# A fixed TensorE order for an attention stage, with its value products one step later

## Chip, cores, metric

One core of a Trainium2 chip runs the whole program. The metric is the device time of one execution in microseconds (us). Below, PE is TensorE, DVE VectorE, ACT ScalarE, POOL GpSimd, and SP the engine that issues the DMAs.

## What is computed

Attention with a causal window of 128 over 4 batches, 8 heads, 576 positions of width 64; then a mixture of 8 experts whose gate is normalised over rows and columns eight times; then a two-layer network with a leaky rectifier. Cut to the stage that the change touches:

```python
scores = q @ k.T / 8 + bias          # per batch and head; bias = -slope[h] * distance
scores = where(0 <= distance < 128, scores, -1e9)
attn = exp(scores - max) ; attn = attn / (attn.sum(-1) + 1e-9)
x = (attn @ v) laid out as (2304, 512)
P = softmax-like gate of x @ w_gate  # 2304 x 8
out = sum over e of P[:, e] * (relu(x @ w1[e]) @ w2[e])
```

## The kernel before

The 2304 tokens are 18 tiles of 128. Attention takes 36 **steps**: tile i, heads 0 to 3 (`quad` 0), then heads 4 to 7 (`quad` 1). Steps are numbered s = 0 to 35, so tile i has steps 2i and 2i+1. A step has four pieces of TensorE work, named here by a letter; all of it is fp32, and the profile shows each fp32 product as two instructions where it uses half of the array.

- **S**, `scores` (L238): four products of 64 rows, eight instructions. Heads of odd and even number lie in the upper and the lower 64 partitions, so that two products that follow each other use different halves of the array's rows. DVE then adds the bias and finds the minimum (L243), ACT does the exponential (L247).
- **T**, `probs_T` (L273): eight transposes of 128 by 128 into two PSUM tiles `pt`; ACT copies each to SBUF as `pb` (L275).
- **V**, `values` (L288): eight products with `v`, sixteen instructions, whose outputs alternate between the lower and the upper 64 partitions. After `quad` 1, DVE multiplies the tile's sums by the inverses and writes `acc[i]` (L296).
- **R**, the second half of `inverses` (L260), once per tile: the inverse row sums are spread over partitions by sixteen instructions, and ACT copies them to `rb` (L263).

In program order a step s issues S of step s+1, then some jobs of a list `fill`, then T of step s (and R at `quad` 1), more of `fill`, and V of step s. `PAIRS` groups the tiles: pairs 0, 1 and 2 are tiles 0 to 3, 4 to 7 and 8 to 11. When a pair's four tiles are done, its `acc` tiles are added and split into two fp16 parts (`XP[p]`, by ACT at L427 and POOL at L428 and L474), and `fill` gets its fourteen products with the first weights (`a_steps`, L702, six instructions each), its gate products (`logits`, L327) and, for pairs 0 and 1, its fourteen products with the second weights (`b_steps`, L819). The same list holds, in steps 0 to 7, the preparation of the first chunk of both weights, W[0][0] and W[1][0]: the largest magnitude (`largest`, four ACT squares each, L550), a scale factor for it (`scale_jobs`: small DVE operations and two small PE products that share one PSUM bank with the other factors), the scaling on ACT (L553), and seven fp16 splits with four sums between them (`whole`: ACT L427, POOL L428 and L577). The k-th product of `a_steps` needs split k of W[0][0], and from the third product on also the sums and the last split of `XP[p]`.

The order on every engine is made by the framework at build time: it takes instructions by program order as their inputs come ready in its own timing of the kernel, and each engine then runs its list in order. So the TensorE order of before is not the program's: pieces are broken up and mixed. An explicit edge without a semaphore (`add_manual_dep` with `NoSync`) forces one instruction behind another in that list.

After step 35 come the inputs of pairs 3 and 4, the gate, and for the remaining 1700 us the products of all chunks.

Of the kernel before, what the change touches and what calls it, by code (L numbers as in the profile page):

```python
# [13 lines left out]
AF = mybir.ActivationFunctionType  # L14
ALU = mybir.AluOpType
# [11 lines left out]
FIRST = (0, 1, 3)  # L27
# [4 lines left out]
def attn_moe_kernel(  # L32
# [81 lines left out]
    pools = {}  # L114

    anchors = {}

    def anchor():
        ins = nc.cur_bb.bb.instructions[-1]
# [93 lines left out]
    def load_v(i):  # L213
        v_t = ap3.tile([P, DM], F32, tag="v", name="v_t")
        nc.sync.dma_start(v_t, v[i * P:(i + 1) * P, :])
        st[i]["v"] = v_t
# [6 lines left out]
    def scores(i, quad):  # L223
        c = st[i]
        kb, qs = c["kb"], c["qs"]
        W = P * len(kb)
        c0 = 2 * P - W
        mn = ap2.tile([P, 4], F32, tag="mn", name="mn")
        if quad == 0:
            c["sm"] = ap2.tile([P, H], F32, tag="sm", name="sm")  # L230
        sm = c["sm"]
        s = [ps_s.tile([P, 2, 2 * P], F32, tag="s", name="s") for _ in range(2)]
        e = [ap1.tile([P, 2, 2 * P], F32, tag="e", bufs=5, name="e") for _ in range(2)]
        c[quad] = dict(e=e)
        for n in range(2):
            for r in range(2):
                h = 4 * quad + 2 * n + r
                nc.tensor.matmul(s[r][:, n, 0:W], qs[64 * r:64 * r + 64, h // 2, :],  # L238
                                 c["k"][64 * r:64 * r + 64, h // 2, 0:W], start=True, stop=True)
        for n in range(2):  # L240
            for r in range(2):
                h = 4 * quad + 2 * n + r
                nc.vector.tensor_tensor_reduce(  # L243
                    out=e[r][:, n, 0:W], in0=s[r][:, n, 0:W], in1=c["bias"][:, c0:], scale=2.0 ** (-8.0 * (h + 1) / H),
                    scalar=float(2**41), op0=ALU.add, op1=ALU.min, accum_out=mn[:, 2 * n + r:2 * n + r + 1],
                )
                nc.scalar.activation(  # L247
                    out=e[r][:, n, 0:W], in_=e[r][:, n, 0:W], func=AF.Exp, bias=mn[:, 2 * n + r:2 * n + r + 1],
                    scale=-1.0, accum_out=sm[:, h:h + 1],
                )  # L250

    def inverses(i):

        c = st[i]
        sm = c["sm"]
        nc.scalar.activation(out=sm, in_=sm, func=AF.Copy, bias=EPS)
        nc.vector.reciprocal(out=sm, in_=sm)
        rt = ps_t.tile([P, NP, P], F32, tag="pt", name="rt")
        for h in range(H):
            nc.tensor.matmul(rt[64 * (h % 2):64 * (h % 2) + 64, h // 2, :], sm[:, h:h + 1].to_broadcast([P, D]), ident,  # L260
                             start=True, stop=True)
        rb = c["rb"] = ap1.tile([P, NP, P], F32, tag="rb", name="rb")
        nc.scalar.activation(out=rb, in_=rt, func=AF.Copy)  # L263

    def probs_T(i, quad):
        c = st[i][quad]
        nb = len(st[i]["kb"])
        c["pb"] = []
        for r in range(2):
            pt = ps_t.tile([P, 2, 2, P], F32, tag="pt", name="pt")  # L270
            for n in range(2):
                for b in range(nb):
                    nc.tensor.transpose(pt[:, n, b, :], c["e"][r][:, n, b * P:(b + 1) * P], ident)  # L273
            pb = ap3.tile([P, 2, 2, P], F32, tag="pb", name="pb")
            nc.scalar.activation(out=pb[:, :, 0:nb, :], in_=pt[:, :, 0:nb, :], func=AF.Copy)  # L275
            c["pb"].append(pb)

    def values(i, quad):
        kb = st[i]["kb"]
        if quad == 0:  # L280
            st[i]["o"] = ps_o.tile([P, NP, P], F32, tag="o", name="o")
        o = st[i]["o"]
        pb = st[i][quad]["pb"]
        for n in range(2):
            for b, j in enumerate(kb):
                for r in range(2):
                    h = 4 * quad + 2 * n + r
                    nc.tensor.matmul(  # L288
                        o[64 * r:64 * r + 64, h // 2, :],
                        st[j]["v"][:, h * D:(h + 1) * D],  # L290
                        pb[r][:, n, b, :],
                        start=(b == 0), stop=(b == len(kb) - 1),
                    )
        if quad == 1:
            p = max(p for p, (t0, n) in enumerate(PAIRS) if t0 <= i)
            nc.vector.scalar_tensor_tensor(out=accT[i], in0=o, scalar=xin[p].sr[:, 0:1], in1=st[i]["rb"],  # L296
                                           op0=ALU.mult, op1=ALU.mult)
# [18 lines left out]
    def logits(p):  # L316

        t0, n = PAIRS[p]
        lp = ps_a.tile([P, 2, n, 2 * E], F32, tag="s1", name="lp")

        first = [(0, wgs, 0), (1, wgs, 2)]
        second = [(0, wgs, 0), (2, wgs, 2), (5, wgn, 0)]
        for s, terms in enumerate((first, second)):
            for k in range(n):
                todo = [(o, w, k0, i) for o, w, k0 in terms for i in range(4)]
                for m, (o, w, k0, i) in enumerate(todo):
                    nc.tensor.matmul(lp[:, s, k, :], XP[p][:, o, i // 2, i % 2, k * P:(k + 1) * P], w[:, k0 + i // 2, :],  # L327
                                     start=(m == 0), stop=(m == len(todo) - 1))
        back = small.tile([P, 1], F32, tag="lb", bufs=1, name="lb")
        nc.scalar.activation(out=back, in_=xin[p].sr[:, 1:2], func=AF.Copy, scale=srg[:, 1:2])  # L330
        to = Pm[:, t0:t0 + 2 * n, :].rearrange("p (s k) e -> p s k e", s=2)
        nc.scalar.activation(out=to, in_=lp[:, :, :, 0:E], func=AF.Copy, scale=back)
        nc.vector.scalar_tensor_tensor(out=to, in0=lp[:, :, :, E:2 * E], scalar=back, in1=to, op0=ALU.mult, op1=ALU.add)
# [105 lines left out]
    class Inputs:  # L439
# [18 lines left out]
        def largest(self, k):  # L458
            nc.vector.tensor_reduce(out=self.mx[:, k:k + 1], in_=acc[self.t0 + k], axis=AX.X, op=ALU.max,
                                    apply_absolute_value=True)  # L460
# [75 lines left out]
    class Weights:  # L536
# [9 lines left out]
            nc.sync.dma_start(self.raw, chunks[self.ci][self.which].rearrange("(k p) f -> p k f", p=P))  # L546

        def largest(self, k):
            junk = stg.tile([P, FC], BF16, tag="junk", bufs=1, name="junk")
            nc.scalar.activation(out=junk, in_=self.raw[:, k], func=AF.Square, accum_out=self.mx[:, k:k + 1])  # L550

# [1 line left out]
            nc.scalar.activation(out=self.raw[:, k], in_=self.raw[:, k], func=AF.Copy, scale=self.sr[:, 0:1])  # L553

        def scale(self):
            jobs = [lambda k=k: self.largest(k) for k in range(KT)] + scale_jobs(self.mx, KT, self.sr, squares=True)
            jobs += [lambda k=k: self.scaled(k) for k in range(KT)]
            if self.which == 1:
                jobs.append(self.back)
            return jobs  # L560
# [106 lines left out]
    def a_steps(ci, p):  # L667
# [6 lines left out]
        def step(g, j, d):  # L674
# [22 lines left out]
            for f in range(nf):  # L697
                ft = g * nf + f
                i = 0
                for kk in range(2):  # L700
                    for wp, xp in ((0, 0), (0, 1), (1, 0)):
                        nc.tensor.matmul(d[b][:, f, :], t[:, wp, kk, ft * P:(ft + 1) * P], XP[p][:, o, kk, xp, :],  # L702
                                         start=(i == 0 and f == 0 and j in FIRST), stop=(i == 5), skip_group_check=True)
                        i += 1
            ps = d[b].rearrange("p f t -> p (f t)")

# [91 lines left out]
    def b_steps(ci, p):  # L798
# [5 lines left out]
        def step(tt, j, d):  # L804
# [11 lines left out]
            for ft in range(2):  # L816
                h, f = Ht[ci, p, ft]
                for hp, wp in ((0, 0), (0, 1), (1, 0)):
                    nc.tensor.matmul(ps, h[:, o, hp, f, tt * P:(tt + 1) * P], w[:, wp, ft, :],  # L819
                                     start=(i == 0 and j in FIRST), stop=(i == 5), skip_group_check=True)  # L820
                    i += 1
            t, half = ((ta, 0), (ta, 0), (ta, 1), (tb, 1), (tb, 1), (ta, 1), (tb, 0))[j]
            dst = acc[t][:, half * HF:(half + 1) * HF]
# [64 lines left out]
    def filling(left):  # L888
        for f in [fill.pop(0) for _ in range(min(-(-len(fill) // max(left, 1)), len(fill)))]:
            if f is not None:  # L890
                f()
            tick()

    for s, (i, quad) in enumerate(steps):
# [11 lines left out]
        if s + 1 < len(steps):  # L906
            if quad == 1 and i + 2 < NTILE:
                load_qk(i + 2)
            if quad == 0 and 2 <= i + 1 < NTILE:
                load_v(i + 1)  # L910
            scores(*steps[s + 1])
        if quad == 0 and i + 5 < NTILE:
            largest_v(i + 5)
        for p, (t0, n) in enumerate(PAIRS):
# [2 lines left out]
        filling(left)  # L917
        if scales:
            scales.pop(0)()
        probs_T(i, quad)  # L920
        if quad == 1:
            inverses(i)
        filling(left - 1)
        if scales:
            scales.pop(0)()
        values(i, quad)
    assert not fill
    for _ in range(8):
        tick()
    actx.close()  # L930
# [150 lines left out]
```

## Time and profile before

| | |
|---|---|
| three runs | 1959.19, 1960.06, 1962.14 us; median 1960.06 |
| the profiled execution | 1959.59 us; its span 1957.8 us |
| PE busy over the span | 1890.2 us (97%), 17725 instructions |
| DVE, ACT, POOL busy | 1320.9 (67%), 1366.5 (70%), 1327.3 us (68%) |
| mean granted TensorE clock | 0.995 |

A busy PE is not a PE at its peak: two products in different halves of the array can run side by side, and the busy time does not tell whether they do. Times inside the kernel count from the span's start.

### The profile page before, as it was taken

The numbers are of one execution on the slowest core, as the hardware profiler recorded it, in microseconds if no ns is written. First come the engines' busy times: TensorE is split into PE (matmuls) and PEld (weight loads), VectorE is DVE, ScalarE is ACT, GpSimd is POOL, SyncE is SP. The second block draws the span as 40 slices with busy tenths as digits, with TensorE's granted clock in tenths as the row PEclk, the third lists the DMA queues.
The fourth block names the chain that finished last, engine by engine and source line by source line (L and its number), as shares of the span: only waits on it lengthen the run. The fifth ranks groups of instructions, "written<-read, shape, count | busy, mean of one in ns | idle before, by whom it ended". The sixth has DMA issues, their size and how long they took to land.

```text
span 1957.8 us, 45103 instructions
## 1 busy us (share of the span) xinstructions
PE 1890.2 (97%) x17725; PEld 1626.5 (83%) x17725; DVE 1320.9 (67%) x3604; ACT 1366.5 (70%) x3123; POOL 1327.3 (68%) x1142
## 2 busy tenths in 40 slices
PE   8999988999999999999999999999999998999998
PEld 6777667888898888889888888889889877889897
DVE  6444466676776767677676767666666777677876
ACT  7977666776767666676767676676666778776764
POOL 3843275868787786878677686775767686666743
PEclk9999999999999999999999999999999999999999
DMA  8432001120211211120111112101000000001001
GB/s 269 125 87 71 12 12 55 39 62 32 82 47 47 66 39 55 39 82 28 66 65 40 55 39 66 44 2 45 23 23 23 23 23 23 24 22 44 2 28 71
DMA packets 57861, 97.80 MB, mean 50 GB/s; under 512 B 3632, under 2 KB 22064, under 8 KB 57648
## 3 DMA queue, kind: packets, MB, share of 16 engines
q1 hardware_dynamic: 57648, 94.92, 14.9%
q8 instruction: 138, 2.26, 0.5%
q14 instruction: 75, 0.61, 0.1%
HBM read 81.81 MB, written 13.11 MB: 48 GB/s over the span
## 4 chain that ended last, share of the span: by engine, by line
PE 78%; ACT 7%; DVE 5%; DMA 5%; POOL 3%; issue 2%; POOLq 0%; SPq 0%; ACTq 0%; DVEq 0%
PE t L819 35%; PE s L702 21%; PE sq L702 15%; DMA raw<-in_moe_w_dram 3%; PE s L238 2%; PE o L288 2%; PE pt L273 1%; ACT junk L550 1%; POOL h L775 1%; DVE s L731 1%; PE rt L260 1%; ACT raw L553 1%; ACT w L427 1%; ACT e L247 1%; ACT xp L427 1%
## 5 line engine op out<-in xcount | busy, mean ns | idle before, releaser
L819 PE MATMUL t<-w,h 128*128 128x256 f16 x7560 | 985.1, 273 | 22.9 <-ACT part L829 10.3
L702 PEld LDWEIGHTS <-w 128*128 128x128 f16 x8400 | 759.1, 98 | 120.3 <-issue 35.0
L819 PEld LDWEIGHTS <-h 128*128 128x128 f16 x7560 | 730.2, 98 | 125.6 <-issue 33.9
L702 PE MATMUL s<-xp,w 128*128 128x256 f16 (+1 forms) x4908 | 620.3, 263 | 20.3 <-ACT q L726 10.4
L832 DVE SCALAR_TENSOR_TENSOR acc<-t,pu,acc 128x256 f32<-128x256 f32 x864 | 407.9, 479 | 220.3 <-PE t L819 173.3
L775 POOL TENSOR_TENSOR h<-s,h 128x1024 f16<-128x1024 f32 x180 | 388.2, 2157 | 136.8 <-ACT h L772 95.7
L702 PE MATMUL sq<-xp,w 128*128 128x256 f16 (+1 forms) x3492 | 447.5, 262 | 6.2 <-ACT q L714 4.5
L830 POOL TENSOR_TENSOR acc<-acc,part 128x256 f32<-128x256 f32 x324 | 235.6, 729 | 292.9 <-ACT part L829 260.6
L428 POOL TENSOR_TENSOR w<-raw,w 128x512 f16<-128x512 f32 x240 | 277.7, 1168 | 42.3 <-ACT w L427 41.9
L731 DVE SCALAR_TENSOR_TENSOR h<-sq,h 128x512 f16<-128x512 f32 (+1 forms) x348 | 190.6, 552 | 82.4 <-ACT h L756 47.6
L829 ACT ACTIVATE part<-t,pu 128x256 f32<-128x256 f32 x324 | 152.5, 471 | 109.0 <-PE t L819 100.1
L772 ACT ACTIVATE h<-s 128x1024 f16<-128x1024 f32 x180 | 189.6, 1053 | 42.2 <-DVE s L731 41.3
L718 DVE SCALAR_TENSOR_TENSOR sq<-sq,q 128x256 f32<-128x256 f32 x348 | 148.4, 427 | 72.0 <-PE sq L702 57.0
L714 ACT ACTIVATE q<-s 128x256 f32<-128x256 f32 x366 | 138.3, 379 | 73.0 <-PE s L702 60.4
L427 ACT ACTIVATE w<-raw 128x512 f16<-128x512 f32 x240 | 148.2, 628 | 8.3 <-PE t L819 6.0
L731 DVE SCALAR_TENSOR_TENSOR s<-sq,s 128x256 f32<-128x256 f32 x348 | 145.1, 417 | 2.1
L750 ACT ACTIVATE h<-sq 128x512 f16<-128x512 f32 x174 | 103.2, 593 | 55.4 <-PE t L819 28.9
L731 DVE SCALAR_TENSOR_TENSOR s<-sq,q 128x256 f32<-128x256 f32 x348 | 130.3, 416 | 12.4 <-ACT q L726 10.6
L550 ACT ACTIVATE junk<-raw 128x512 bf16<-128x512 f32 x160 | 100.2, 626 | 48.2 <-DMA raw<-in_moe_w_dram 47.1
L718 DVE SCALAR_TENSOR_TENSOR sq<-s,q 128x256 f32<-128x256 f32 x174 | 74.5, 428 | 86.6 <-ACT q L714 78.2
L756 ACT ACTIVATE h<-sq 128x256 f16<-128x256 f32 x174 | 65.9, 379 | 65.1 <-DVE sq L718 58.2
L553 ACT ACTIVATE raw<-raw,sr 128x512 f32<-128x512 f32 x160 | 102.4, 714 | 3.8 <-DVE sr L422 3.4
(137 smaller groups left out, 1785.8 us busy)
## 6 DMA issues: line engine op xcount, KB each, us to landing
raw<-in_moe_w_dram SPq DMA_DIRECT2D x32, 1024.0 KB, 5.1
k_t<-in_k_dram SPq DMA_DIRECT2D x16, 512.0 KB, 3.8
raw<-in_moe_w_in_dram SPq DMA_DIRECT2D x16, 512.0 KB, 3.6
raw<-in_moe_w_out_dram SPq DMA_DIRECT2D x16, 512.0 KB, 3.5
q_t<-in_q_dram SPq DMA_DIRECT2D x18, 256.0 KB, 3.7
v_t<-in_v_dram SPq DMA_DIRECT2D x18, 256.0 KB, 2.7
acc<-in_v_dram SPq DMA_DIRECT2D x18, 256.0 KB, 6.6
out_dram<-acc SPq DMA_DIRECT2D x18, 256.0 KB, 2.0
```

The source lines that it names most:

```text
L427: nc.scalar.activation(out=hi, in_=src, func=AF.Copy)
L428: nc.gpsimd.tensor_tensor(out=lo, in0=src, in1=hi, op=ALU.subtract)
L702: nc.tensor.matmul(d[b][:, f, :], t[:, wp, kk, ft * P:(ft + 1) * P], XP[p][:, o, kk, xp, :], start=(i == 0 and f == 0 and j in FIRST), sto ...
L714: nc.scalar.activation(out=q[:, k], in_=ps, func=AF.Copy, scale=CS)
L718: nc.vector.scalar_tensor_tensor(out=block(k), in0=ps, scalar=CS, in1=q[:, k], op0=ALU.mult, op1=ALU.add)
L731: nc.vector.scalar_tensor_tensor(out=out, in0=in0, scalar=sc, in1=in1, op0=op0, op1=op)
L772: nc.scalar.activation(out=h[:, 3:7, 0, :], in_=d["s"], func=AF.Copy)
L775: nc.gpsimd.tensor_tensor(out=h[:, 3:7, 1, :], in0=d["s"], in1=h[:, 3:7, 0, :], op=ALU.subtract)
L819: nc.tensor.matmul(ps, h[:, o, hp, f, tt * P:(tt + 1) * P], w[:, wp, ft, :], start=(i == 0 and j in FIRST), stop=(i == 5), skip_group_chec ...
L829: nc.scalar.activation(out=part, in_=ps, func=AF.Copy, scale=s)
L830: nc.gpsimd.tensor_tensor(out=dst, in0=dst, in1=part, op=ALU.add)
L832: nc.vector.scalar_tensor_tensor(out=dst, in0=ps, scalar=s, in1=dst, op0=ALU.mult, op1=ALU.add)
```

## The change

Every PE instruction of the attention stage is tied to the one before it, in program order, until the last V (`kept`; the small products of `scale_jobs` are not tied). V moves one step later: step s now issues S of step s+1, then R of the tile before (at `quad` 0, split off as `spread_inverses`), V of step s-1, `fill`, T of step s, and `fill`. The load of the next `v` tile moves behind that V. Of the two `pb` copies of a step DVE makes the second. The largest magnitudes of the first chunk of weights are found by DVE instead of ACT squares.

```diff
+    in_order = [None]
+    def kept(ins):
+        if in_order:
+            if in_order[0] is not None:
+                tc.add_manual_dep(ins.ins, in_order[0],
+                                  mybir.DependencyInfo(mybir.DependencyClass.NoSync, mybir.DependencyReason.DATA),
+                                  reason="in order")
+            in_order[0] = ins.ins.name
...
+    def spread_inverses(i):
+        c = st[i]
+        sm = c["sm"]
         rt = ps_t.tile([P, NP, P], F32, tag="pt", name="rt")
...
-            nc.scalar.activation(out=pb[:, :, 0:nb, :], in_=pt[:, :, 0:nb, :], func=AF.Copy)
+            if r == 0:
+                nc.scalar.activation(out=pb[:, :, 0:nb, :], in_=pt[:, :, 0:nb, :], func=AF.Copy)
+            else:
+                nc.vector.tensor_copy(pb[:, :, 0:nb, :], pt[:, :, 0:nb, :])
...
         def largest(self, k):
+            if self.ci == 0:
+                nc.vector.tensor_reduce(out=self.mx[:, k:k + 1], in_=self.raw[:, k], axis=AX.X, op=ALU.max,
+                                        apply_absolute_value=True)
+                return
...
-            jobs = [lambda k=k: self.largest(k) for k in range(KT)] + scale_jobs(self.mx, KT, self.sr, squares=True)
+            jobs = [lambda k=k: self.largest(k) for k in range(KT)] + scale_jobs(self.mx, KT, self.sr, squares=self.ci > 0)
...
-            if quad == 0 and 2 <= i + 1 < NTILE:
-                load_v(i + 1)
             scores(*steps[s + 1])
+        if s:
+            if quad == 0:
+                spread_inverses(i - 1)
+            values(*steps[s - 1])
+        if quad == 0 and 2 <= i + 1 < NTILE:
+            load_v(i + 1)
...
-        probs_T(i, quad)
         if quad == 1:
             inverses(i)
+        probs_T(i, quad)
         filling(left - 1)
...
-        values(i, quad)
+    spread_inverses(NTILE - 1)
+    values(*steps[-1])
     assert not fill
+    in_order.clear()
```

The PE instructions of `scores`, `spread_inverses`, `probs_T`, `values`, `logits`, `a_steps` and `b_steps` are each wrapped in `kept(...)`.

## Rows read from the trace of the kernel before

**Rows 1.** The chain that ended last, by engine, whole span.
```profile
PE 78%; ACT 7%; DVE 5%; DMA 5%; POOL 3%; issue 2%; POOLq 0%; SPq 0%; ACTq 0%; DVEq 0%
```

**Rows 2.** Windows: busy us and instructions of each engine, granted clock, DMA share.
```profile
20.00:50.00 30.00, 29.33 (x242) 20.90 (x244) 24.76 (x117) 27.79 (x86) 10.88 (x12) 1.00 0.72 232
50.00:75.00 25.00, 23.42 (x181) 16.67 (x177) 9.27 (x45) 25.00 (x75) 23.91 (x23) 1.00 0.38 108
75.00:232.00 157.00, 156.52 (x1477) 115.70 (x1477) 77.19 (x274) 112.40 (x328) 59.14 (x52) 1.00 0.25 75
```

**Rows 3.** Timeline of PE: start, us, what, instructions merged into one run.
```profile
34.65 1.09 PE L288 MATMUL o<-pb,v_t 128*64 128x128 f32 x16
35.67 1.13 PE L238 MATMUL s<-k_t,qs 64*128 64x256 f32 x8
...
76.25 1.13 PE L238 MATMUL s<-k_t,qs 64*128 64x256 f32 x4
...
79.52 1.09 PE L273 MATMUL pt<-ident,e 128*128 128x128 f32 x8
...
230.19 0.43 PE L288 MATMUL o<-pb,v_t 128*64 128x128 f32 x2
...
230.88 1.09 PE L288 MATMUL o<-pb,v_t 128*64 128x128 f32 x14
```

**Rows 4.** Windows of PE for L238 alone, then L288 alone.
```profile
20.00:232.00 212.00, 58.43 (x264) 1.00 0.33 101
...
20.00:232.00 212.00, 49.14 (x534) 1.00 0.33 101
```

**Rows 5.** Groups by line, first 250 us; then three tiles: ns min/median/max.
```profile
L275 ACT ACTIVATE pb<-pt 128x512 f32<-128x512 f32 x64 | 37.5, 592 | 14.3 <-PE pt L273 13.8 <-PE o L288 0.2
L474 POOL TENSOR_TENSOR sx<-acc,sx 128x256 f32<-128x256 f32 x12 | 9.3, 775 | 0.4
...
L550 ACT ACTIVATE junk<-raw x8: 615/626/630, 16.2 to 25.4; 128x512 bf16<-128x512 f32 x8
...
L221 DVE TENSOR_REDUCE vmx<-acc x18: 622/664/686, 10.7 to 35.1; 128x1 f32<-128x512 f32 x18
...
L296 DVE SCALAR_TENSOR_TENSOR acc<-o,srx,rb x18: 728/750/752, 23.8 to 232.5; 128x512 f32<-128x512 f32 x18
```

**Rows 6.** The chain that ended last, start and us: two stretches' first and last pieces.
```profile
23.77 0.75 DVE acc L296
...
36.92 0.34 DVE e L243
...
37.30 1.10 ACT e L247 x5
...
68.16 0.49 ACT rb L263
```

**Rows 7.** Timelines of DVE, PE and ACT: the first weights' factor, scaling and products.
```profile
20.85 0.13 DVE L394 TENSOR_REDUCE m<-mxw 128x1 f32<-128x4 f32 x1
...
37.09 0.22 PE L402 MATMUL mt<-identb,e 128*1 128x128 bf16 x1
...
42.42 0.16 DVE L422 COPY sr<-st 128x2 f32<-128x2 f32 x1
...
44.11 2.55 ACT L553 ACTIVATE raw<-raw,sr 128x512 f32<-128x512 f32 x4
...
77.31 1.27 PE L702 MATMUL s<-xp,w 128*128 128x256 f16 x10
```

**Rows 8.** Timeline of POOL: the splits of XP[0], first and last but for one tile part.
```profile
50.23 2.13 POOL L428 TENSOR_TENSOR xp<-sx,xp 128x1024 f16<-128x1024 f32 x1 [0.18 <-ACT xp L427]
...
73.83 2.14 POOL L428 TENSOR_TENSOR xp<-sx,xp 128x1024 f16<-128x1024 f32 x1
```

**Rows 9.** Waits of the DMA queue on SP, first 235 us: total, times, longest.
```profile
SPq L215 <- PE o L288: 69.8, 13, 13.2
```

**Rows 10.** Window of all engines just behind the attention stage.
```profile
233.00:247.00 14.00, 9.37 (x83) 6.41 (x81) 7.03 (x15) 10.79 (x25) 10.34 (x9) 0.76 0.01 2
```

More of the change, by code (lines that the diff above doesn't have):

```diff
@@ L237, in scores @@
                 h = 4 * quad + 2 * n + r
-                nc.tensor.matmul(s[r][:, n, 0:W], qs[64 * r:64 * r + 64, h // 2, :],
-                                 c["k"][64 * r:64 * r + 64, h // 2, 0:W], start=True, stop=True)
+                kept(nc.tensor.matmul(s[r][:, n, 0:W], qs[64 * r:64 * r + 64, h // 2, :],
+                                 c["k"][64 * r:64 * r + 64, h // 2, 0:W], start=True, stop=True))
         for n in range(2):
@@ L257, in inverses @@
         nc.vector.reciprocal(out=sm, in_=sm)
+    def spread_inverses(i):
+        c = st[i]
+        sm = c["sm"]
         rt = ps_t.tile([P, NP, P], F32, tag="pt", name="rt")
         for h in range(H):
-            nc.tensor.matmul(rt[64 * (h % 2):64 * (h % 2) + 64, h // 2, :], sm[:, h:h + 1].to_broadcast([P, D]), ident,
-                             start=True, stop=True)
+            kept(nc.tensor.matmul(rt[64 * (h % 2):64 * (h % 2) + 64, h // 2, :], sm[:, h:h + 1].to_broadcast([P, D]), ident,
+                             start=True, stop=True))
         rb = c["rb"] = ap1.tile([P, NP, P], F32, tag="rb", name="rb")
@@ L272, in probs_T @@
                 for b in range(nb):
-                    nc.tensor.transpose(pt[:, n, b, :], c["e"][r][:, n, b * P:(b + 1) * P], ident)
+                    kept(nc.tensor.transpose(pt[:, n, b, :], c["e"][r][:, n, b * P:(b + 1) * P], ident))
             pb = ap3.tile([P, 2, 2, P], F32, tag="pb", name="pb")
-            nc.scalar.activation(out=pb[:, :, 0:nb, :], in_=pt[:, :, 0:nb, :], func=AF.Copy)
+            if r == 0:
+                nc.scalar.activation(out=pb[:, :, 0:nb, :], in_=pt[:, :, 0:nb, :], func=AF.Copy)
+            else:
+                nc.vector.tensor_copy(pb[:, :, 0:nb, :], pt[:, :, 0:nb, :])
             c["pb"].append(pb)
@@ L287, in values @@
                     h = 4 * quad + 2 * n + r
-                    nc.tensor.matmul(
+                    kept(nc.tensor.matmul(
                         o[64 * r:64 * r + 64, h // 2, :],
@@ L292, in values @@
                         start=(b == 0), stop=(b == len(kb) - 1),
-                    )
+                    ))
         if quad == 1:
@@ L326, in logits @@
                 for m, (o, w, k0, i) in enumerate(todo):
-                    nc.tensor.matmul(lp[:, s, k, :], XP[p][:, o, i // 2, i % 2, k * P:(k + 1) * P], w[:, k0 + i // 2, :],
-                                     start=(m == 0), stop=(m == len(todo) - 1))
+                    kept(nc.tensor.matmul(lp[:, s, k, :], XP[p][:, o, i // 2, i % 2, k * P:(k + 1) * P], w[:, k0 + i // 2, :],
+                                     start=(m == 0), stop=(m == len(todo) - 1)))
         back = small.tile([P, 1], F32, tag="lb", bufs=1, name="lb")
@@ L701, in step @@
                     for wp, xp in ((0, 0), (0, 1), (1, 0)):
-                        nc.tensor.matmul(d[b][:, f, :], t[:, wp, kk, ft * P:(ft + 1) * P], XP[p][:, o, kk, xp, :],
-                                         start=(i == 0 and f == 0 and j in FIRST), stop=(i == 5), skip_group_check=True)
+                        kept(nc.tensor.matmul(d[b][:, f, :], t[:, wp, kk, ft * P:(ft + 1) * P], XP[p][:, o, kk, xp, :],
+                                         start=(i == 0 and f == 0 and j in FIRST), stop=(i == 5), skip_group_check=True))
                         i += 1
@@ L818, in step @@
                 for hp, wp in ((0, 0), (0, 1), (1, 0)):
-                    nc.tensor.matmul(ps, h[:, o, hp, f, tt * P:(tt + 1) * P], w[:, wp, ft, :],
-                                     start=(i == 0 and j in FIRST), stop=(i == 5), skip_group_check=True)
+                    kept(nc.tensor.matmul(ps, h[:, o, hp, f, tt * P:(tt + 1) * P], w[:, wp, ft, :],
+                                     start=(i == 0 and j in FIRST), stop=(i == 5), skip_group_check=True))
                     i += 1
```

## Prediction

> **What bounds the kernel now.** I read the chain that ended last first. TensorE holds 78% of it [rows 1], so a time can only come down where PE itself does less, or waits less. Next I read the windows of the stage that the change touches, from 20 us to the end of the last V at 230.88 + 1.02 = 231.9 us [rows 3]. PE is busy nearly all of it, but ACT is busy for all of 50 to 75 us and DVE for 24.8 of the 30 us before [rows 2]. The chain puts this in order: from 23.8 to 37.3 us it runs on DVE without a break, from 37.3 to 68.6 us on ACT [rows 6], and then on PE to the end of the stage.
>
> The busy share hides that PE works badly. On its timeline, S as one run of eight lasts 1.13 us, and so does a run of four [rows 3]. The reader is to see that eight take no longer because neighbours in different halves of the array run side by side; four of one half run one after another. (Each run's last 0.07 us overlap the next run, so 1.06 and 1.02 are what S and V cost.) V as sixteen lasts 1.09 us; split into two and fourteen it costs 0.36 more [rows 3]. By the same measure 264 instructions of S would take 33 x 1.13 = 37 us, and they are busy for 58.4; 534 of V would take 36.4 and are busy for 49.1 [rows 4]. That is 34 us; with 0.07 us off for each of the some 75 needless runs, about 29 us of PE time in this stage goes to broken pairs.
>
> **The change part by part.** *The fixed order.* It gives S and V back their pairs, at most -29 us, on condition that the next instruction in program order is ready when PE gets to it. A step then needs 1.06 (S) + 1.02 (V) + 1.02 (T), and every second step 1.02 for R, which has V's form and count [rows 3]. A product of the fill list, six instructions, I take at 0.75 us: the ten of one run take 1.27 less 0.07 [rows 7], 0.72 for six, and a change of kind comes on top.
>
> *The first hold-up.* The fill list's first products stand in step 8 and the third is the second job of step 9. It needs split 2 of W[0][0] and the sums' split of XP[0]. Before, PE went on with steps 10 to 14 while these were missing; the third product and what follows could start only after POOL's last split at 73.83 + 2.14 = 76.0, and ran from 77.3 [rows 7, 8]. In a fixed order S, T and V wait behind it. So the date of that product sets the rest. The factor of W[0][0] is written at 42.4; its maximum was there at 20.9, but its PE product came only at 37.1 [rows 7], as the one PSUM bank was held by the gate's factor, which DVE finished in the stretch where the chain runs on DVE. So finding the maxima on another engine does not bring the factor forward. With 42.4 kept, scaling takes 2.5 us and the first split half a us: POOL starts at 45.5 and not at 52.4, when the split of XP[0] before it ended [rows 7, 8]. From 50.2 to 76.0 POOL worked off both inputs of pair 0; 2.1 us of it (the first row) can go before, and 3.5 belong to W[1][0], whose first sum and two splits were mixed in. That leaves 20.1 us, so the third product at 65.6. Bounds: 58, if DVE takes the 13 reductions of `v` that it hurried through (0.6 us each, L221 [rows 5]) later and the factor comes 7 us sooner; 84, if POOL takes W[1][0]'s 13 us and DVE's extra work goes in front. I take the value between, nearest to the factor's own row.
>
> *What remains then for PE.* Steps 9 (rest) to 15: twelve first products 9.0, the gate's forty small ones 1.0, fourteen second products 10.5, T 1.0, six steps 18.6, three R 3.1: 43.2. Steps 16 to 23: 24.8 + 4.1 + 21 + 1 = 50.9. Steps 24 to 35, one S fewer: 36.1 + 6.1 + 10.5 + 1 = 53.7. The closing R and V: 2.0. Sum 149.8. Changes of kind, 0.08 us in each of 27 steps: 2.2. Waits: pair 1 meets the third product 4.6 us after its last V, but L296 (0.75), four sums on POOL (0.78 each), an ACT split (about half of POOL's) and 2.14 on POOL [rows 5, 8] make 7.1 with the rest of POOL's queue 7.9, so 3.3 us. The third of the second products meets the same kind of chain twice, 1 us each. Pair 2 has one job to a slot and does not wait. In all 157.3.
>
> *V, R and the inverses moved.* Between T and its V now lie a slot of `fill`, the next S and, at quad 0, R: at least 1.5 us, against 0.6 for a copy [rows 5]. PE waited little for `pb` before, so by itself this gives nothing; in the fixed order it is the cover that keeps V from waiting. What is late next is L296, by about a step, and with it the pair's inputs, which I have counted as the 3.3 us. Without that cover (a copy 1.5 us late in each step) it would cost 36 x 0.5 = 18 us.
>
> *One copy to DVE.* ACT loses 36 of 592 ns, starting 0.48 us apart. DVE's price is not in the trace; the nearest rows are the 512-element reduction from SBUF (622 to 686 ns, L221) and the two-operand L296 that also reads PSUM (750) [rows 5], which I take as its bounds. 0.65 is nearer to the first, having one operand too: 23 us in all. DVE is busy 77 of 157 us after 75 us [rows 2], so there it is hidden. Before 37 us it is not: some eight copies.
>
> *The maxima on DVE.* ACT loses eight squares of some 0.75 us with their readout, 6 us, which all lie before 26 us [rows 5], where ACT did not set the chain. DVE gains eight of 0.6 us, 4.8, in the stretch where it did. With the copies that is up to 9.6 us more for DVE before 37 us, against 7.8 of hurried reductions that can give way. I count nothing and keep both ends in the bounds of the date above.
>
> *The loads.* The load of `v` waits for a V, already 13 times and up to 13.2 us [rows 9], with the loads of q and k and of `acc` behind it in SP's queue. The 18 loads now start about a step later and are needed three steps later, so nothing; if that cover were gone, S of a tile would wait a DMA's time.
>
> *The clock.* A hold-up of ten us or more idles PE. Behind the stage, where PE idles in small pieces, the granted clock is 0.76 of 2.4 GHz over 14 us [rows 10]: 6.7 us at 1.2 GHz, 3.4 us of work lost. I take 3.5. The Trainium skill, "TensorE: Matmul & The Clock Gate", Part 1, says that the array falls to half rate after idling and has to be warmed by activity; this row agrees. By the rule each later wait could add as much again; against it, in 75 to 232 us the granted clock stayed at 1.00 [rows 2].
>
> *Behind the stage* the list is the same and starts earlier by what the stage gains. Two and a half second products of pair 2 that PE had done before 232 us move behind it, where PE idles. Orders made anew at build time may shift the rest by some 3 us either way, the spread of the three runs.
>
> Sum: 65.6 + 157.3 + 3.5 = 226.4 against 231.9, -5.5 us: 1959.6 - 5.5 = 1954.1 for the profiled execution, 0.5 below the median of the runs, so **1954**.
>
> **The rivals.** *PE never waits.* The factor comes so early that the third product runs at its place, near 50 us; then 50 + 157.3 = 207, 25 us sooner: 1935. For it: 29 us are there to be had, and POOL is idle for 19 of the 30 us before 50. Against it: the factor's row at 42.4 and 20 us of POOL work behind it. *The hold-up decides*, ending slower. POOL takes W[1][0] before the last split of XP[0], as its place in the program says, and PE stands until 75 to 84: 79 + 157.3 + 3.5 = 240, 8 us later: 1968. It decides from a third product later than 71 us (231.9 - 160.8). For it: nothing else may pass that product; against it: POOL mixed the two before, with the last split ahead of five of W[1][0]'s seven. Two more losses of 3.4 us at half clock, behind later waits, belong here too: the forecast's date then ends at 1961. *Given back.* The pairs come back and the waits eat them, or the order of the rest shifts: 1957 to 1963.
>
> **How the numbers follow.** The forecast's case (third product at 58 to 68, 1947 to 1956) 0.30; PE never waits 0.20; hold-up or clock 0.28; given back 0.22. A measurement of this kernel tells some 0.2% (4 us) from no change. Faster 0.50, same 0.22, slower 0.28. The range runs from short of the first rival's end, 1934, to 84 us for the third product, 1972. The forecast's own range is 1947 to 1958.
>
> **What would show it.** S should stand in runs of eight and V in runs of sixteen, at 1.1 us each, throughout. The first L702 runs should be followed by a PE wait, on POOL (w or xp), that ends at 60 to 70 us; a granted clock below 1.00 behind it. The sr copy at L422 should stay near 42 us. The last V should end at 226 us. I am wrong if runs of eight last 2 us (no pairs in program order), if the factor moves by more than 7 us, if PE waits for `pb` or for DVE at L243 in the later steps, or if the difference arises behind the stage.

## The result, and the profile after

The changed kernel takes 1974.57 us (median of 5 runs, 1971.29 to 1979.98); the kernel before takes 1959.19 us beside it (5 runs). The ratio is 1.0082, with a 95% interval of 1.0058 to 1.0107: **slower by 0.8%**, where 1954 us was forecast, with a range up to 1972. The profiled execution took 1979.98 us, the longest of the five; its span is 1978.2 us, 20.4 longer than before, where the two medians lie 15.4 us apart.

The loss lies in the attention stage. The last V ends at 249.45 + 1.02 = 250.5 us and not at 231.9, 18.6 us later. In the 14 us behind it the granted clock is 0.76, as in [rows 10], and from 400 to 1900 us PE is busy for 1467.4 us against 1469.3 before.

Windows of the kernel before, from the start to its last V (busy us and instructions of PE, its weight loads, DVE, ACT, POOL; granted clock, DMA share, GB/s):

```profile
0.00:231.90 231.90, 223.47 (x1954) 162.74 (x1954) 118.75 (x474) 176.09 (x522) 99.62 (x108) 1.00 0.39 119
20.00:100.00 80.00, 77.75 (x664) 56.37 (x665) 48.86 (x199) 72.16 (x215) 52.01 (x48) 1.00 0.52 164
100.00:231.90 131.90, 131.42 (x1233) 96.80 (x1231) 62.26 (x235) 93.04 (x271) 41.91 (x37) 1.00 0.22 63
```

The same windows of the changed kernel, and the stretch around the third product:

```profile
0.00:250.50 250.50, 198.44 (x1967) 154.59 (x1968) 142.83 (x522) 156.80 (x473) 100.90 (x109) 0.93 0.35 110
20.00:100.00 80.00, 49.28 (x400) 35.98 (x400) 40.48 (x154) 46.80 (x132) 45.98 (x43) 0.79 0.43 140
100.00:250.50 150.50, 136.73 (x1495) 109.61 (x1496) 91.09 (x320) 102.60 (x313) 49.22 (x43) 0.99 0.23 68
...
75.00:100.00 25.00, 13.62 (x108) 10.50 (x109) 7.12 (x20) 10.04 (x24) 13.01 (x12) 0.68 0.26 85
```

This is the account of the change. PE's work up to the last V fell by 25.0 us (223.5 to 198.4). Its standing time, the window less the busy time, rose by 43.6 (8.4 to 52.1): by 28.5 us between 20 and 100 us (2.2 to 30.7), by 13.3 behind 100 us (0.5 to 13.8), and by 1.9 before 20 us. The sum, -25.0 + 43.6, is the 18.6.

The work fell because the pairs came back. Windows of the changed kernel for the lines of S and of V alone, which answer to [rows 4]:

```profile
20.00:250.50 230.50, 38.85 (x256) 23.68 (x256) 0.92 0.30 93
...
20.00:250.50 230.50, 37.44 (x528) 30.18 (x528) 0.92 0.30 93
```

S takes 152 ns an instruction against 221, V 71 against 92. PE's timeline around the third product (start, us, what, count; in brackets the time PE stood before it, and for whom), with the last V:

```profile
64.69 1.49 PE L725 MATMUL s<-xp,w 128*128 128x256 f16 x6
66.11 1.70 PE L249 MATMUL s<-k_t,qs 64*128 64x256 f32 x8
67.73 1.09 PE L307 MATMUL o<-pb,v_t 128*64 128x128 f32 x16
68.76 0.83 PE L725 MATMUL s<-xp,w 128*128 128x256 f16 x6
82.66 0.37 PE L725 MATMUL s<-xp,w 128*128 128x256 f16 x1 [13.07 <-ACT xp L446]
85.86 1.23 PE L725 MATMUL s<-xp,w 128*128 128x256 f16 x5 [2.84 <-POOL xp L447]
86.88 1.91 PE L289 MATMUL pt<-ident,e 128*128 128x128 f32 x8
88.59 2.74 PE L725 MATMUL s<-xp,w 128*128 128x256 f16 x12
...
97.47 1.47 PE L725 MATMUL s<-xp,w 128*128 128x256 f16 x12 [0.88 <-ACT q L749]
...
249.45 1.04 PE L307 MATMUL o<-pb,v_t 128*64 128x128 f32 x16
```

S stands in eights and V in sixteens, but for a few single breaks. But the third product gets its last input at 85.86 us, and all of PE stands behind it. The runs after the wait are at the lower of the two clock levels (1.2 and 2.4 GHz): twelve instructions, two first products, take 2.74 us at 88.59 and 1.47 at 97.47, and the window has 0.68. POOL, which made that input, did not rest from 48.49 us on; its timeline:

```profile
48.49 2.27 POOL L447 TENSOR_TENSOR w<-raw,w 128x512 f16<-128x512 f32 x2 [0.81 <-ACT w L446]
...
63.35 1.18 POOL L447 TENSOR_TENSOR w<-raw,w 128x512 f16<-128x512 f32 x1
64.47 1.29 POOL L600 TENSOR_TENSOR raw<-raw 128x512 f32<-128x512 f32 x1
65.69 3.40 POOL L447 TENSOR_TENSOR w<-raw,w 128x512 f16<-128x512 f32 x3
...
70.41 2.13 POOL L447 TENSOR_TENSOR xp<-sx,xp 128x1024 f16<-128x1024 f32 x1
...
73.11 1.27 POOL L600 TENSOR_TENSOR t<-raw 128x512 f32<-128x512 f32 x1
74.33 1.27 POOL L600 TENSOR_TENSOR raw<-raw 128x512 f32<-128x512 f32 x1
...
76.24 1.26 POOL L600 TENSOR_TENSOR raw<-raw,t 128x512 f32<-128x512 f32 x1
77.46 1.16 POOL L447 TENSOR_TENSOR w<-t,w 128x512 f16<-128x512 f32 x1
78.57 2.27 POOL L447 TENSOR_TENSOR w<-raw,w 128x512 f16<-128x512 f32 x2
...
81.47 2.27 POOL L447 TENSOR_TENSOR w<-raw,w 128x512 f16<-128x512 f32 x2
83.69 2.12 POOL L447 TENSOR_TENSOR xp<-sx,xp 128x1024 f16<-128x1024 f32 x1
```

The row at 83.69 is the last split of `XP[0]`, which before started at 73.83 [rows 8]. All four sums (L600) and seven splits of W[1][0], the second weights, which nobody needs yet, stand ahead of it from 64.47 on (two of the three splits at 65.69 are theirs): 12.7 us by the starts of the rows. The first tiles were late too. DVE's timeline at the start:

```profile
16.21 2.45 DVE L569 TENSOR_REDUCE mxw<-raw 128x1 f32<-128x512 f32 x4
...
19.17 1.85 DVE L569 TENSOR_REDUCE mxw<-raw 128x1 f32<-128x512 f32 x3
21.07 0.66 DVE L569 TENSOR_REDUCE mxw<-raw 128x1 f32<-128x512 f32 x1
21.66 0.40 DVE L254 CUSTOM_DVE_ANT_0 e<-s,dist 128x256 f32<-128x256 f32 x1
...
30.26 0.74 DVE L315 SCALAR_TENSOR_TENSOR acc<-o,srx,rb 128x512 f32<-128x512 f32 x1
```

The bias (L254) of the next step waits behind the eight maxima until 21.66, and the first `acc` comes at 30.26 against 23.8 [rows 5]; the fourth, which closes pair 0, starts at 63.76 against 55.93.

### The profile page after: what moved, and what is told of

Its sections match the earlier page's. It is cut to its first block, busy times and chain, and to the rows that moved or that the text cites. A ratio compares the mean times of both kernels' runs of the same rounds, so it can differ in the third digit from the quotient of the medians.

```text
span 1978.2 us, 45093 instructions
## 1 busy us (share of the span) xinstructions
PE 1863.1 (94%) x17725; PEld 1616.3 (82%) x17725; DVE 1342.7 (68%) x3644; ACT 1345.8 (68%) x3071; POOL 1326.4 (67%) x1142
## 3 DMA queue, kind: packets, MB, share of 16 engines
q1 hardware_dynamic: 57648, 94.92, 14.6%
## 5 line engine op out<-in xcount | busy, mean ns | idle before, releaser
L447 POOL TENSOR_TENSOR w<-raw,w 128x512 f16<-128x512 f32 x240 | 277.7, 1167 | 44.9 <-ACT w L446 44.5
L754 DVE SCALAR_TENSOR_TENSOR s<-sq,q 128x256 f32<-128x256 f32 x348 | 129.9, 414 | 12.5 <-ACT q L749 10.6
L741 DVE SCALAR_TENSOR_TENSOR sq<-s,q 128x256 f32<-128x256 f32 x174 | 74.4, 427 | 86.5 <-ACT q L737 78.1
L573 ACT ACTIVATE junk<-raw 128x512 bf16<-128x512 f32 x152 | 95.3, 627 | 52.9 <-DMA raw<-in_moe_w_dram 51.9
```

The costliest lines, as they stand in the source:

```text
L447: nc.gpsimd.tensor_tensor(out=lo, in0=src, in1=hi, op=ALU.subtract)
L741: nc.vector.scalar_tensor_tensor(out=block(k), in0=ps, scalar=CS, in1=q[:, k], op0=ALU.mult, op1=ALU.add)
L754: nc.vector.scalar_tensor_tensor(out=out, in0=in0, scalar=sc, in1=in1, op0=op0, op1=op)
```

## The experiments

All are timed against the kernel before, run beside them (its medians: 1958.4 to 1960.7 us). "Work" and "standing" are PE's busy time up to the end of the last V, and the rest of that time. All edits are to the changed kernel, but for e2.

| run | edit | us, median | ratio (95%) | work | standing | last V ends |
|---|---|---|---|---|---|---|
| before | | 1959.19 | | 223.5 | 8.4 | 231.9 |
| after | the whole change | 1974.57 | 1.0058 to 1.0107 | 198.4 | 52.1 | 250.5 |
| e1 | no order | 1962.75 | 1.0012 to 1.0030 | 225.9 | 11.6 | 237.5 |
| e2 | the order alone, on the kernel before | 1996.02 | 1.0175 to 1.0203 | 204.5 | 66.3 | 270.8 |
| e3 | maxima on ACT | 1970.36 | 1.0037 to 1.0063 | 199.3 | 42.7 | 242.0 |
| e4 | both copies on ACT | 1971.17 | 1.0052 to 1.0081 | 194.8 | 50.5 | 245.3 |
| e5 | order from step 16 on | 1959.57 | 0.9984 to 1.0006 | 212.1 | 22.5 | 234.6 |
| e6 | one half's four S first | 1982.75 | 1.0094 to 1.0129 | 200.4 | 55.1 | 255.5 |
| e7 | W[1][0] behind XP[0] on POOL | 1965.94 | 1.0019 to 1.0040 | 199.7 | 40.2 | 239.9 |
| e8 | pair 0's products 16 slots later | 1966.20 | 1.0012 to 1.0037 | 201.9 | 42.7 | 244.6 |
| e9 | R and V between S's fours | 1992.97 | 1.0163 to 1.0190 | 230.8 | 39.6 | 270.4 |
| e10 | e7 and e3 | 1968.66 | 1.0040 to 1.0067 | 197.4 | 44.9 | 242.3 |
| e11 | e10 and e8 | 1968.60 | 1.0044 to 1.0069 | 196.9 | 43.7 | 240.6 |
| e12 | e11, four tiles' copies on ACT | 1966.28 | 1.0032 to 1.0063 | 198.8 | 40.5 | 239.3 |
| e13 | S, T, V, R tied; the rest free | 1949.18 | 0.9946 to 0.9969 | 206.7 | 24.6 | 231.3 |
| e14 | e13 and e3 | 1954.32 | 0.9969 to 0.9986 | 210.9 | 21.3 | 232.2 |
| e15 | ties inside each piece alone | 1949.75 | 0.9943 to 0.9973 | 216.9 | 11.7 | 228.6 |
| e16 | e14 and e7 | 1954.54 | 0.9966 to 0.9988 | 204.1 | 24.6 | 228.7 |

**The parts of the change: e1 to e4.** e1 leaves out the ties:

```diff
-    in_order = [None]
+    in_order = []
```

> The changed kernel without the edges between PE instructions: V stays one step later, DVE keeps its copies and maxima, and the order on PE is again free. Theory 1, the hold-up (the fixed order makes S, T and V wait behind the third product, which starts at 85.9 us): the wait of 16 us goes, the broken pairs come back, and the time is that of before within 6 us, 1953 to 1966. Theory 2, early load on DVE (maxima and copies delay the first tiles: the first L296 moved from 23.8 to 30.3 us): most of the loss stays, 1970 to 1978.

Met, as the first theory said. The work is back at 225.9 us and the standing down to 11.6: both come from the order. What is left of the change by itself costs 0.2%.

e2 is the kernel before with every PE instruction tied as in the change, V in its old place, copies and maxima on ACT. Against the changed kernel, the places of V and R:

```diff
-        if s:
-            if quad == 0:
-                spread_inverses(i - 1)
-            values(*steps[s - 1])
...
+            spread_inverses(i)
...
+        values(i, quad)
```

> The kernel before with the fixed order alone: V stays in its old place, ACT makes both copies and the maxima. Theory 1: slower than before by 10 to 35 us (1970 to 1995), as the hold-up stays and V now also waits in every step for copies that lie directly before it. Theory 2: 1950 to 1962, since DVE has no more work than before.

It came 1 us above the first theory's range. In e2 PE waits 23.5 us for `pb` ahead of R and 21.4 ahead of V; its last V ends 184.2 us after the third product, in the changed kernel 164.6, and in e4, which has the later V and both copies on ACT as e2, 163.1. The cover of the later V is worth some 20 us in a fixed order.

e3 and e4 take one part back each:

```diff
-            if self.ci == 0:
-                nc.vector.tensor_reduce(out=self.mx[:, k:k + 1], in_=self.raw[:, k], axis=AX.X, op=ALU.max,
-                                        apply_absolute_value=True)
-                return
```

> The changed kernel with the first weights' maxima back on ACT squares. Theory 1: the date of the third product hangs on POOL and moves by 5 us at most, so 1969 to 1977. Theory 2: the 5 us of reductions between 16 and 22 us go from DVE, the first L296 comes back to 24 to 26 us and the time falls to 1962 to 1968.

```diff
-            if r == 0:
-                nc.scalar.activation(out=pb[:, :, 0:nb, :], in_=pt[:, :, 0:nb, :], func=AF.Copy)
-            else:
-                nc.vector.tensor_copy(pb[:, :, 0:nb, :], pt[:, :, 0:nb, :])
+            nc.scalar.activation(out=pb[:, :, 0:nb, :], in_=pt[:, :, 0:nb, :], func=AF.Copy)
```

> The changed kernel with both copies of a step on ACT again. Theory 1: ACT has room (its busy share fell), so within 4 us of the changed kernel, 1971 to 1979, with some more waits of V for pb. Theory 2: DVE loses some 0.6 us a step and the time falls by 3 to 6 us.

With the maxima on ACT the first `acc` starts at 24.21, as theory 2 said, and the third product at 77.48: the maxima cost 8.4 us of its date, more than theory 1 allowed, and some 4 us of the time, though the two intervals still overlap. POOL's timeline of e3 shows how:

```profile
48.70 1.16 POOL L447 TENSOR_TENSOR w<-raw,w 128x512 f16<-128x512 f32 x1 [4.88 <-ACT w L446]
...
71.22 2.28 POOL L447 TENSOR_TENSOR w<-raw,w 128x512 f16<-128x512 f32 x2
...
74.07 1.28 POOL L596 TENSOR_TENSOR raw<-raw 128x512 f32<-128x512 f32 x1
75.29 2.14 POOL L447 TENSOR_TENSOR xp<-sx,xp 128x1024 f16<-128x1024 f32 x1
```

POOL begins the weights no sooner than in the changed kernel (48.70 against 48.49) and hardly rests, but only two splits and one sum of W[1][0] stand ahead of the last split of `XP[0]`, 3.5 us in place of 12.7. So the 8.4 us are POOL's order. That the later tiles led the build to that order is argued, not shown. What the copies cost, 3 us by the medians, the intervals don't tell from nothing.

**Where the order begins: e5.** The list is untied until step 16.

```diff
-    in_order = [None]
+    in_order = []
...
+        if s == 16:
+            in_order.append(None)
```

> The changed kernel with the order on PE free until step 16 and fixed from there: pair 0's products, among them the third, are passed over as before. Theory 1 (the end is the third product's date plus 164 us, only because nothing may pass it): no wait of more than 3 us at the first products, S and V whole from some 100 us on, some 12 to 17 us less than the kernel with no fixed order at all (1962.8): 1945 to 1952. If the loss lies in the fixed order anywhere (small waits in all steps): 1960 to 1972.

Missed: no gain over the kernel before. From 99.9 to 128.3 us its timeline has products with the weights and small ones of the gate and the factors, and no S, T, V or R: the tied steps stand. That the tie's first product with the weights waits for a PSUM bank that pair 0's products hold is argued, not shown.

**What a pair is: e6 and e9.** e6 turns the two loops in `scores` round, so that the four instructions of one half stand together, then those of the other:

```diff
-        for n in range(2):
-            for r in range(2):
+        for r in range(2):
+            for n in range(2):
```

> The changed kernel with the loops of S exchanged: the two products of one half of the array follow each other, the work and the number of instructions are the same. If the pairs are worth what the timeline says (1.06 us for each S), steps 11 to 34 behind the third product cost some 24 x 1.06 = 25 us more, less what waits take up: 1990 to 2002. If runs of eight at 1.1 us have another cause: 1972 to 1978.

S still stands in eights of 1.14 us. So alternating neighbours are not what counts. The time falls between the two ranges. Whether it is above the changed kernel's is not settled: the ratios are 0.3% apart, with intervals that overlap. The third product comes at 86.06 us, as there, and the rest takes 5 us longer.

e9 has e6's loops, and issues R and V of the step between the two fours:

```diff
+            if r == 1 and between is not None:
+                between()
```

> The changed kernel, with the spread of the inverses and the value products of a step issued between the first four and the last four of the score products, inside the fixed order. If eight score products run at 1.13 us because the two fours stand next to each other, and a four alone takes as long as the eight (some 1.06 us, as S x4 groups took in the kernel before), each step pays about 1.06 us more from the moment pair 0's products set the end: 20 to 28 steps, so 1993 to 2003 us. If the engine pays for products one by one and adjacency is not what counts, 1972 to 1980.

Met, at the lower end of the first range. PE's timeline of e9, and its window of S alone:

```profile
203.31 1.13 PE L251 MATMUL s<-k_t,qs 64*128 64x256 f32 x4
204.37 1.09 PE L278 MATMUL rt<-ident,sm 128*64 128x128 f32 x16
205.29 1.04 PE L309 MATMUL o<-pb,v_t 128*64 128x128 f32 x16
206.27 1.13 PE L251 MATMUL s<-k_t,qs 64*128 64x256 f32 x4
```
```profile
20.00:270.40 250.40, 74.57 (x260) 44.27 (x260) 0.92 0.28 86
```

A four costs what an eight costs. S takes 74.6 us where the changed kernel has 38.9. The last V ends 19.9 us later, 5.7 of it in the date of the third product (91.51), and the measured time is 18 us longer: the profile's lengths of the broken pairs are real time.

**The hold-up: e7, e8, e10 to e12.** e7 holds W[1][0]'s sums and splits behind the last split of `XP[0]`:

```diff
+    def behind(job):
+        def run():
+            with tc.issue_after(pin[0]):
+                job()
+        return run
+    held_back = [behind(job) for job in W[1][0].whole()] + [W[0][1].load, W[1][1].load, None]
```

(`pin[0]` is that split.)

> The changed kernel with POOL's work on the second weights of the first chunk (four sums, seven splits, 13 us) tied behind the last split of pair 0's inputs; on the fill list it stands between the first products. Theory 1: the third product's date falls from 85.9 to 71 to 74 us and the end with it, 12 to 15 us less: 1959 to 1963. Theory 2 (the date hangs on the late accumulators of the slowed first tiles alone): the date stays at 82 us or later and the time at 1971 to 1977.

The third product comes at 74.42 instead of 85.86, near the first theory's date, and the last V ends 10.6 us sooner: POOL's order was that much of it. The time, 1965.94, is 3 us above that theory's range. e8 puts 16 list entries that issue nothing ahead of pair 0's products:

```diff
-                    fill += xin[p].parts(1) + a_steps(0, p) + [lambda p=p: logits(p)]
+                    fill += xin[p].parts(1) + [None] * (16 if p == 0 else 0) + a_steps(0, p) + [lambda p=p: logits(p)]
```

> The changed kernel with sixteen empty jobs ahead of pair 0's first products, which puts them some three steps later in the program's order, three jobs to a slot from there; all work is the same. Theory 1: PE does three steps of S, T and V (10 to 12 us) where it stood, and the time falls by 8 to 13 us: 1961 to 1967. If PE could do no more in that time, as the copies or POOL hold it: within 4 us of the changed kernel.

Met: PE works in the hole, and the stage ends 5.9 us sooner. Then the edits together: e10 has those of e7 and e3, e11 that of e8 too, and e12 makes both copies of the first four tiles on ACT:

```diff
-            if r == 0:
+            if r == 0 or i < 4:
```

> W[1][0]'s sums and splits on POOL held back behind XP[0]'s last split, and the first weights' maxima back on ACT, both on the changed kernel. Theory 1 (the end of the stage is the third product's date plus about 164 us, and the two causes of the late date add): date 68 to 72, stage end 232 to 237, time 1956 to 1963. Theory 2 (the dates do not add, since the late accumulators alone set XP[0]'s splits): date near 74 and 1964 to 1968.

> As the run before, with 16 empty jobs ahead of pair 0's products, so that their date in the order comes later than their data. Theory 1 (the rest of the stage after the date is PE's own work, and score and value steps that ran during the wait are taken out of it): PE hardly stands, stage end 224 to 232, time 1948 to 1958. Theory 2 (each four products moved behind the date must be made up at the end, at half clock or without cover): 1960 to 1968.

> As the run before, with both probability copies of the first four tiles on ACT, so that VectorE accumulates the first tiles sooner. If VectorE's copies delay the first accumulators: 2 to 5 us less than the run before, 1945 to 1957. If ACT, which makes exponentials too, then sets the first tiles: no gain, or 1 to 4 us more.

All three missed the range of their first theory, and this was the finding. In e10 the fourth `acc` comes 6.8 us sooner than in e7 (57.32 against 64.13), but the last split of `XP[0]` starts at 72.12 against 72.25, and the third product at 74.30, as the second theory said. The two edits do not add, as both take the same work, that of W[1][0], from ahead of the split: in both runs POOL works without a rest from some 48 to some 71 us, and then waits 1.2 and 1.6 us for ACT's part. In e11 PE does not wait at the third product (75.97 us), and still stands 43.7 us. Its windows, with the columns as above:

```profile
20.00:100.00 80.00, 60.51 (x584) 46.09 (x584) 52.20 (x190) 61.78 (x182) 51.78 (x46) 0.94 0.49 154
100.00:240.60 140.60, 124.75 (x1317) 99.43 (x1314) 80.62 (x282) 90.37 (x275) 44.69 (x40) 0.96 0.22 65
```

PE stands 19.5 us in the first window and 15.9 in the second, in small waits: 7.3 us for `rb`, 4.9 for `pb`, 4.6 for ACT's part of the second products are the largest groups behind the start. The hold-up was the largest wait, but without it the order finds others.

**Which ties cost: e13 to e16.** e13 unties only the products with the weights and the gate's products:

```diff
-                        kept(nc.tensor.matmul(d[b][:, f, :], t[:, wp, kk, ft * P:(ft + 1) * P], XP[p][:, o, kk, xp, :],
+                        nc.tensor.matmul(d[b][:, f, :], t[:, wp, kk, ft * P:(ft + 1) * P], XP[p][:, o, kk, xp, :],
...
-                    kept(nc.tensor.matmul(ps, h[:, o, hp, f, tt * P:(tt + 1) * P], w[:, wp, ft, :],
+                    nc.tensor.matmul(ps, h[:, o, hp, f, tt * P:(tt + 1) * P], w[:, wp, ft, :],
```

> The changed kernel with S, T, V and R tied in one order as before, but the products with the first and second weights and the gate's products left untied, so that attention steps may go on past a product whose data are late. If the loss lies in tying the late products to the attention (PE stands 52 us to the last V instead of 8), PE's work stays near 200 us and its idle time falls to 10 to 25 us: stage end 210 to 230, time 1937 to 1958. If the loss lies in the order of the attention pieces themselves (the waits of 20 to 50 us), idle stays above 35 us and the time above 1966.

Met: 1949.18 us, 0.4% faster than the kernel before and, by the two ratios, 1.2% faster than the changed one. PE's timeline of e13, then POOL's last split of `XP[0]`, then its window to the last V:

```profile
55.44 0.28 PE L725 MATMUL s<-xp,w 128*128 128x256 f16 x1
...
75.68 2.08 PE L249 MATMUL s<-k_t,qs 64*128 64x256 f32 x8
77.69 1.93 PE L307 MATMUL o<-pb,v_t 128*64 128x128 f32 x16
...
83.70 0.38 PE L725 MATMUL s<-xp,w 128*128 128x256 f16 x2
...
89.09 1.27 PE L725 MATMUL s<-xp,w 128*128 128x256 f16 x10
```
```profile
86.03 2.14 POOL L447 TENSOR_TENSOR xp<-sx,xp 128x1024 f16<-128x1024 f32 x1
```
```profile
0.00:231.30 231.30, 206.72 (x1961) 154.08 (x1962) 141.01 (x522) 156.40 (x473) 101.20 (x109) 0.97 0.39 119
```

The split is as late as in the changed kernel, and even 2.3 us later. But between 55.4 and 83.7 us no product with the weights stands in PE's list; S, T, R and V of the steps run there. The edit frees the first, the second and the gate's products at once; how much each of them had cost was not tried. Standing falls from 52.1 to 24.6 us, and 16.7 of the 25.0 us of saved work stay. The stage ends where it did before; by 235 us PE has done 198 instructions of second products against 186, some 1.5 us, and between 400 and 1900 us 31 instructions more, some 3 us. The rest of the 9 us was not followed.

> As e13_att_only, with the first weights' maxima back on ACT. If DVE's maxima still delay the first tiles, which still pass through a fixed order: 2 to 5 us less than e13_att_only, as between the changed kernel and e3_act_max. If the late products alone made that delay matter: within 2 us of it.

Missed: 5 us more than e13, not less, and why is open. Putting the maxima back does not help once the products are free, though the third product then comes 5.9 us sooner (83.21 against 89.09).

e15 ties each piece only within itself (the chain is cut where a piece begins):

```diff
+    def fresh():
+        if in_order:
+            in_order[0] = None
```

> As e13_att_only, but each piece (the eight S, the sixteen V, R, the eight T) tied within itself alone, not to the next piece. In the built order many pieces are then broken into one and three products by others. If adjacency is what saves PE's work, PE's work to the last V is above 212 us, near that of the untied kernel (226), and the time 1955 to 1966; if the order within a piece is enough, PE's work stays near 200 us and the time at or below e13_att_only.

Work as the first theory said (216.9, well above 200), but the time came out better than it said: the standing (11.7 us) pays it back, and e15 ends level with e13.

> As e14_att_act_max, with W[1][0]'s work on POOL behind XP[0]'s last split as in e7_w1_late. If the third product's date no longer sets the rest once attention may pass it: within 3 us of e14_att_act_max. If it does: 3 to 8 us less.

Within 0.3 us of e14, with the third product 3.2 us sooner (80.01): its date no longer shows in the time. (The ends of the stage in e13 to e16 do not rank their times; what the order made anew does behind the stage differs by some 5 us and was not followed.)

## Why the prediction was wrong

**What failed: the size of "the first hold-up".** The date of the third product was put at 65.6 us, and is 85.86, beyond even its bound of 84. The stage's forecast end was 5.5 us sooner and came 18.6 later; of the 24.1 us between, 20.3 are this date. Its sum was 45.5 for POOL's start and 20.1 for POOL's work, and both terms were too small:

- POOL starts at 48.49, 3.0 us later. The factor hardly moved (43.5 against "near 42"). But ACT scales only from 44.38 on, and does exponentials and a copy before the first split. [Rows 7] had shown the same lag, 42.42 to 44.11, and the sum left it out.
- POOL then works 37.3 us without a rest, 17.2 more. Of these 12.7 are W[1][0]. The estimate took its 3.5 us out of the row of before and put nothing in their place; in the changed kernel all of it stands ahead, and e7, which holds it back, moves the date by 11.4 us. The other 4.5 us are, on balance, sums and a split of pair 0 that POOL had done before the weights and now does behind its start.

"I count nothing" for DVE's maxima was wrong too: e3 puts them at 8.4 us of the date. These are not a second cause to be added, as e3's POOL list and e10 show, but the same W[1][0] work, which with the maxima on DVE stands ahead of the split.

**The rival "the hold-up decides" came true**, by the mechanism that it named, POOL taking W[1][0] first. It said 1968 from a date of 79; the date was 6.9 us later still, and the time 6.6 us longer. The date from which it decides, 71 us, becomes 67 with the measured rest (231.9 - 164.6): e7, at 74.4, ended 8.0 us behind the kernel before.

**Near, partly by luck: the rest after the date.** 157.3 us for the list and 3.5 for the clock were forecast to the last V, 160.8 in all, and 164.6 were measured. But two errors offset each other. PE stands 14.6 us in that stretch where the waits were put at 5.3; pair 1's wait at the third product was right (3.7 us against 3.3), and the others are mostly small waits for ACT and DVE at the products with the weights. And PE's work is 150.0 us where 155.5 were forecast with the clock. Nor is the 164 a constant: with the product's date moved in the order, e8 has 157.5, and e11, with the same list and no wait there, 164.6; e6 has 169.4 and e9 178.9. So a calculation by one date alone, which the prediction and my first experiments both made, holds only near the list for which it was worked out.

**Right: the broken pairs**, 29 us at most; 25.0 us less work, and e9 shows that they are real time. Their cause was told too narrowly. What counts is not that neighbours alternate, but that both halves' work stands together, with nothing between (e6, e9).

**Right, nearly: the copy on DVE**, forecast at 0.65 us. Its group in the changed kernel mixes 32 copies of 512 elements, 678 ns each, with four of 256, 418 ns:

```profile
L294 DVE COPY pb<-pt 128x512 f32<-128x512 f32 (+1 forms) x36 | 23.4, 649 | 42.2 <-PE pt L289 41.5 <-ACT e L258 0.7
```

**Right in size: the cover of the later V**, 18 us forecast, some 20 by e2. The forecast's 0.5 us a step has no row behind it, so this is luck in part. **Right: the loads.** The wait of [rows 9] fell from 69.8 to 22.3 us; that of the loads of k behind S rose from 57.5 to 127.9, but no S waits for a load behind the start.

**The clock** was charged in the right place: window and runs fell to the lower level after the wait. The forecast's sum left out that short waits bring it too: the clock is 0.83 in 20 to 50 us, where PE stood for 2 to 3 us at a time, and was 1.00 there before [rows 2]. The Trainium skill, "TensorE: Matmul & The Clock Gate", Part 1, says that the array drops to half rate after idling; both windows agree.

**What was left out altogether.** The prediction asked where the one late product stops PE. It did not ask what the greedy order had been paying its broken pairs for. It had 8.4 us of standing in 232 us, with 223.5 of work; the fixed order has the work of 198 and no way round any late input. e11 and e12, with the hold-up nearly gone, still stand over 40 us and are still slower than the kernel before. e13 settles the cause: with the late products free, the split comes 2.3 us later still, and the stage ends 19.2 us sooner than in the changed kernel.

## What to carry to other kernels

Before fixing an engine's order, list the inputs that come late in it: behind each, the whole engine stands, not only its piece. Tie what gains from standing together, and leave free what waits for other engines; here that is the difference between +0.8% and -0.4%. And when a gain is taken from a busy engine, set up the account of work and standing at once (here 25 us won, 44 lost); the end of the stage alone shows neither.

## What the runs showed of the hardware

Two groups of products in different halves of the array run side by side whether they alternate or follow each other as fours: eight instructions of S take 1.13 and 1.14 us in the two orders, and a four between other work takes the same 1.13 (e6, e9). That a broken four costs a whole eight shows in the measured time too, 1992.97 us against 1974.57, which was more than I had expected of a modelled end.
